# Attention with a mixer and an MLP on one core: which loads are issued in the opening, where the abs-max scans stand, and how the first normalized block is transposed

## The chip, the cores and the metric

The kernel runs on one core of a Trainium2 chip. The metric is the device time of one execution in microseconds. Five engines work beside each other: TensorE (PE, its weight loads PEld), VectorE (DVE), ScalarE (ACT), GpSimd (POOL) and SyncE (SP), whose sequencer here only issues DMAs. Each engine runs its instructions strictly in the order in which they stand in the program, and waits on semaphores where an operand comes from another engine or a DMA.

## The reference, cut to what matters

```python
xn = _layernorm(x)                       # x: 2048 tokens x 576
q = xn @ wq                              # 32 heads of 128
k, v = k_cache[:, :, -512:], v_cache[:, :, -512:]   # 16 key/value heads, two query heads each
p = softmax(q @ k.T * 128**-0.5)
s = concat_heads(p @ v) @ wo
h = gelu(_layernorm(xn) @ w1)            # four groups, shifted by 1, -1, 2, -2 tokens
x1 = xn + shifted(h) @ w2
g = silu(x1 + gelu(_layernorm(x1) @ w3) @ w4)
out = x + s * g
```

## The kernel before, in words

The program has two phases. The first (attention and mixer, lines 120 to 463) goes over four blocks of 512 tokens, and in each over 32 heads: 128 units u = 32·block + head. For every unit, `stage_q` projects the query (five matmuls of 128x512 into the tile `psq`, L242, copied to `qT` by ACT, L245), `stage_s` makes the scores of four key chunks (matmul `sc`, L254; exponential `pT` on ACT, L256; three PSUM buffers for `sc`), `stage_v` multiplies with the values (16 matmuls of 128x129 into `po`, two PSUM buffers, L269) and lets DVE divide by the sum (L272, L273) into `o`, which has three buffers, and `stage_t` transposes `o` by a DMA into `oT` (L280). In a step u the code calls `stage_q(u+1)`, `stage_s(u)`, `stage_v(u-1)`, `stage_t(u-2)`, and then what the table `fill` holds for that step: `at(u, fn)` puts it there. Through `fill` go the output projection of the block before (`wo_units`, 128 + 128 matmuls in the first steps of a block), the second layernorm (`ln2`), the mixer's first matmul and its gelu (`b1`: five times five matmuls `ph`, L334, with DVE and ACT work), its second (`b2`), the layernorm of the next block (`ln1`) and its DMA transposes (`tr1`), and loads.

The query weights pass through two buffers `wq_b`, each for four units: load j waits until the units that use the buffer's old slab have been projected. Keys (transposed by DMA, `kT`) and values (`v_sb`) are loaded once per key/value head, and stay. So do `wo_sb` (4.6 MB), `w1_sb` and `w2_sb`.

A guard runs beside this: the largest absolute value of every key head (`k_max`, L230, 16 reduces on DVE) and of each of the eight `wq` slabs (L438, 8 reduces of 128x2560) is combined by `finish_flag` into a flag, and a slow exact softmax follows if the bound is exceeded. It isn't with these inputs.

In the opening the code issues, on SP, four tiles of `x`, the first `wq` slab, keys and values of heads 0 and 1, the second slab, head 2; a GpSimd queue gets all of `wo` (L199) and then `w1` and `w2` (L204 to L213). `ln1(0)` and `tr1(0, .)` follow, then `stage_q(0)`.

The order within an engine is not the order of the code alone. A scheduler in the tile layer puts the instructions of each engine in order by its own estimate of when their operands are there; it may move a DVE reduce that the code has in step 20 ahead of the layernorm of the opening, if it reckons DVE idle there. What it made of the two programs is shown with the change.

The second phase (the MLP over four blocks, lines 466 on) loads its own weights and is not touched by the change.

Of the kernel before, what the change touches and what calls it, by code (L numbers as in the profile page):

```python
# [14 lines left out]
I32 = mybir.dt.int32  # L15

# [10 lines left out]
def kernel(  # L27
# [95 lines left out]
    with ExitStack() as actx:  # L123
# [16 lines left out]
        mx = res.tile([P, 8 + Hkv], FP32, name="mx")  # L140

# [40 lines left out]
        load_x(0, nc.sync)  # L182
        for w in wq_b:
            nc.gpsimd.memset(w[DR:, NF, :], 0.0)
        for w in xn_b + [xnn_b]:
            nc.gpsimd.memset(w[:, :, D:], 0.0)
        load_wq(0)
        load_kv(0)
        load_kv(1)
        nc.gpsimd.memset(v_sb[:, :, :, Dh:VW], 1.0)  # L190
        load_wq(1)
        load_kv(2)
# [4 lines left out]
        def load_wo():  # L197
            for h0 in range(0, Hq, 8):
                nc.gpsimd.dma_start(out=wo_sb[:, h0:h0 + 8, :],  # L199
                                    in_=A_wo[h0 * P:(h0 + 8) * P, :].rearrange("(h p) d -> p h d", p=P))  # L200

        def load_w12():
            for g in range(4):
# [7 lines left out]
                                    in_=B_w1[NF * P:D, g * c4 + P:(g + 1) * c4])  # L211
                nc.gpsimd.dma_start(out=w2_sb[:, g, :], in_=B_w2[g * c4:g * c4 + P, :])
# [23 lines left out]
        def stage_q(u):  # L236
            qb, h = divmod(u, Hq)
            w = wq_b[(u // 4) % NWQ]
            hh = h % 4
            psq = ps_pq.tile([P, QB], FP32, name="psq", tag="pq")  # L240
            for kc in range(NDC):
                nc.tensor.matmul(psq[:, :], lhsT=w[:, kc, hh * Dh:(hh + 1) * Dh], rhs=xnT_b[qb % 2][:, kc, :],  # L242
                                 start=(kc == 0), stop=(kc == NDC - 1))
            qT = qT_pool.tile([P, QB], BF16, name="qT")
            nc.scalar.activation(out=qT[:, :], in_=psq[:, :], func=ACT.Copy)  # L245
            qT_t[u] = qT
# [159 lines left out]
        for b in range(NB):  # L406
# [15 lines left out]
            if b + 1 < NB:  # L422
                at(base + 4, lambda b=b: load_x(b + 1, nc.gpsimd))
# [5 lines left out]
        at(2, load_wo)  # L429
        at(4, load_w12)  # L430
        for g in range(Hkv):
            if g + 3 < Hkv:
                at(2 * g, lambda g=g: load_kv(g + 3))
            at(2 * g + 2, lambda g=g: k_max(g))
        for j in range(2, NB * 8):
            at(4 * (j - 1), lambda j=j: load_wq(j))
        for j in range(8):
            at(4 * j + 1, lambda j=j: nc.vector.tensor_reduce(  # L438
                out=mx[:, j:j + 1], in_=wq_b[j % NWQ][:].rearrange("p a b -> p (a b)"), axis=AX.X, op=ALU.max,
                apply_absolute_value=True))  # L440
# [266 lines left out]
```

## Time and profile before

| | us |
|---|---|
| median of 3 runs | 969.01 (967.73 to 970.4) |
| the profiled execution: its own time | 967.13 |
| its span, from the first to the last instruction | 965.4 |
| TensorE busy | 866.0 (90%) |
| VectorE busy | 354.5 (37%) |
| ScalarE busy | 447.5 (46%) |
| first matmul | at 45.27 |

TensorE is the engine that is busy most, over all of the span but its opening. A busy share is read by stage: the windows view below gives it for each block of 32 units, and the waits view says what ended an engine's idle times.

### The profile page before, as it was taken

What the parts mean: (1) busy time and instruction counts of PE and PEld (TensorE: products, weight loads), DVE (VectorE), ACT (ScalarE), POOL (GpSimd) and SP (SyncE); (2) the same over time, 40 slices, a digit from 0 to 9 for tenths busy, and PEclk for the clock granted to TensorE, in tenths of its full rate; (3) what the DMA queues carried; (4) which work ended last, traced back from release to release, by engine and by line L of the source; (5) the groups of instructions that cost most, each with busy time, mean ns of one, the idle gap of its engine ahead of it and who ended that gap; (6) DMA issues with size and microseconds to landing.
All of it is one profiled execution on the core that took longest, in us unless ns stands there. A gap on an engine that the chain in (4) does not pass through costs nothing.

```text
span 965.4 us, 15852 instructions
## 1 busy us (share of the span) xinstructions
PE 866.0 (90%) x6356; PEld 468.6 (49%) x6356; DVE 354.5 (37%) x1145; ACT 447.5 (46%) x842; POOL 44.5 (5%) x84
## 2 busy tenths in 40 slices
PE   0168998999998999999999999957999999999996
PEld 0035554556555556556546555433444444444453
DVE  3567954212765212765203744300205104203012
ACT  0056686635767635768526767102223223224510
POOL 3510000000000000000000000010000000000000
PEclk9998999999999999999999999987999999999998
DMA  9985353303348303336403232439403103201001
GB/s 271 202 142 120 79 112 58 83 12 78 83 99 150 83 12 80 82 95 138 77 8 108 59 107 64 140 114 299 133 1 120 32 1 94 58 1 50 1 14 40
DMA packets 165648, 84.38 MB, mean 87 GB/s; under 512 B 122176, under 2 KB 163392, under 8 KB 165568
## 3 DMA queue, kind: packets, MB, share of 16 engines
q1 hardware_dynamic: 162160, 73.11, 32.9%
q0 software_dynamic: 3408, 10.19, 3.7%
q8 instruction: 52, 0.85, 0.4%
q14 instruction: 28, 0.23, 0.1%
HBM read 47.07 MB, written 9.44 MB: 59 GB/s over the span
## 4 chain that ended last, share of the span: by engine, by line
PE 71%; ACT 12%; SPq 5%; DMA 5%; issue 3%; DVE 3%; POOL 0%; DVEq 0%; ACTq 0%; POOLq 0%
PE ph L527 16%; PE pm L536 13%; PE psq L242 12%; PE pswo L296 12%; ACT qT L245 6%; PE po L269 6%; ACT pT L256 5%; PE sc L254 5%; DMA wq_b<-in_A_wq_dram 3%; SPq L178 2%; PE ph L334 2%; PE psx L370 2%; PE pr L537 2%; PE pswr L307 2%; DMA kT<-in_A_k_cache_dram 1%
## 5 line engine op out<-in xcount | busy, mean ns | idle before, releaser
L256 ACT ACTIVATE pT<-sc 128x512 bf16<-128x512 f32 x512 | 266.1, 609 | 5.7 <-PE sc L254 5.5
L242 PE MATMUL psq<-xnT_b,wq_b 128*128 128x512 bf16 x640 | 164.7, 386 | 45.8 <-DMA xnT_b<-xn_b 45.3
L527 PE MATMUL ph<-x1nT,w_s 128*128 128x512 bf16 x720 | 175.2, 384 | 15.0 <-DMA x1nT<-xm_b 15.0
L269 PEld LDWEIGHTS <-pT 128*128 128x128 bf16 x2048 | 140.9, 99 | 89.8 <-DVE o L273 25.6
L269 PE MATMUL po<-v_sb,pT 128*128 128x129 bf16 x2048 | 163.6, 222 | 20.2 <-DVE o L273 20.2
L254 PE MATMUL sc<-qT,kT 128*128 128x512 bf16 x512 | 155.3, 385 | 6.6
L530 ACT ACTIVATE h<-ph 128x512 bf16<-128x512 f32 x144 | 85.6, 596 | 156.1 <-PE ph L527 156.1
L536 PE MATMUL pm<-w_s,h 128*128 128x512 bf16 x576 | 155.0, 380 | 0.1
L245 ACT ACTIVATE qT<-psq 128x512 bf16<-128x512 f32 x128 | 76.4, 597 | 164.8 <-PE psq L242 164.7
L272 DVE RECIPROCAL ri<-po 128x2 f32<-128x2 f32 x256 | 42.9, 168 | 241.7 <-PE po L269 240.2
L296 PE MATMUL pswo<-wo_sb,oT 128*128 128x512 bf16 x512 | 113.2, 379 | 2.1 <-ACT s_out L299 2.1
L273 DVE TENSOR_TENSOR o<-po,ri 128x256 bf16<-128x256 f32 x256 | 107.7, 422 | 11.8 <-DMA oT<-o 5.4
L242 PEld LDWEIGHTS <-wq_b 128*128 128x128 bf16 x640 | 60.1, 99 | 105.2 <-issue 49.9
L527 PEld LDWEIGHTS <-w_s 128*128 128x128 bf16 x720 | 64.3, 99 | 90.8 <-DMA x1nT<-xm_b 15.1
L537 PE MATMUL pr<-w_s,h 128*128 128x64 bf16 x576 | 108.0, 193 | 0.0
L536 PEld LDWEIGHTS <-h 128*128 128x128 bf16 x576 | 56.2, 98 | 67.2
L545 DVE TENSOR_TENSOR bs<-pm,x 128x512 f32<-128x512 f32 x16 | 10.7, 686 | 205.3 <-PE pm L536 150.3
L296 PEld LDWEIGHTS <-oT 128*128 128x128 bf16 x512 | 49.4, 98 | 59.7 <-issue 2.9
L254 PEld LDWEIGHTS <-kT 128*128 128x128 bf16 x512 | 50.8, 99 | 47.5 <-issue 3.8
L537 PEld LDWEIGHTS <-h 128*128 128x128 bf16 x576 | 55.4, 98 | 12.7
L299 ACT ACTIVATE s_out<-pswo 128x512 bf16<-128x512 f32 x16 | 9.6, 597 | 105.4 <-PE pswo L296 105.4
L115 DVE BATCH_NORM_STATS2 ln_st<-x 128x6 f32<-128x288 bf16 x32 | 12.5, 431 | 72.7 <-DMA x<-x_dram 72.7
(77 smaller groups left out, 389.4 us busy)
## 6 DMA issues: line engine op xcount, KB each, us to landing
wq_b<-in_A_wq_dram SPq DMA_DIRECT2D x32, 512.0 KB, 3.9
w_s<-in_B_w_dram SPq DMA_DIRECT2D x9, 576.0 KB, 8.2
wo_sb<-in_A_wo_dram POOLq DMA_DIRECT2D x4, 1152.0 KB, 12.8
w_s<-in_B_w_dram SPq DMA_DIRECT2D x9, 512.0 KB, 7.9
s_dram<-s_out SPq DMA_DIRECT2D x4, 576.0 KB, 3.4
x_dram<-x1o SPq DMA_DIRECT2D x4, 576.0 KB, 3.5
s_b<-s_dram SPq DMA_DIRECT2D x4, 576.0 KB, 5.6
x_b<-in_A_x_dram SPq DMA_DIRECT2D x4, 576.0 KB, 6.3
```

Source lines behind the costliest of these rows:

```text
L242: nc.tensor.matmul(psq[:, :], lhsT=w[:, kc, hh * Dh:(hh + 1) * Dh], rhs=xnT_b[qb % 2][:, kc, :], start=(kc == 0), stop=(kc == NDC - 1))
L245: nc.scalar.activation(out=qT[:, :], in_=psq[:, :], func=ACT.Copy)
L254: nc.tensor.matmul(sc[:, :], lhsT=kT[:, g, kc * P:(kc + 1) * P], rhs=qT[:, :], start=True, stop=True)
L256: nc.scalar.activation(out=pT[:, :], in_=sc[:, :], func=ACT.Exp, scale=SCALE)
L269: nc.tensor.matmul(po[:, j, :], lhsT=pTs[kc][:, tt * P:(tt + 1) * P], rhs=v_sb[:, g, kc, 0:Dh + 1], start=(kc == 0), stop=(kc == KCH - 1))
L272: nc.vector.reciprocal(out=ri[:], in_=po[:, :, Dh])
L273: nc.vector.tensor_tensor(out=o[:, t0:t0 + 2, :], in0=po[:, :, 0:Dh], in1=ri[:].unsqueeze(2).to_broadcast([P, 2, Dh]), op=ALU.mult)
L296: nc.tensor.matmul(st["ps"][:, :], lhsT=oT_t[qb * Hq + h][:, tt, :], rhs=wo_sb[:, h, 0:M0], start=(h == 0), stop=(h == Hq - 1))
L527: nc.tensor.matmul(ph[:, :], lhsT=w3[:, kc, f0:f0 + P], rhs=x1nT[b % 2][:, kc, :], start=(kc == 0), stop=(kc == NDC - 1))
L530: nc.scalar.activation(out=h3[:, :], in_=ph[:, :], func=ACT.Gelu_apprx_tanh)
L536: nc.tensor.matmul(pm[tt][:, :], lhsT=lhsT, rhs=w4[:, fc % WS, 0:M0], start=(fc == 0), stop=(fc == FC - 1))
L537: nc.tensor.matmul(pr[:, tt, :], lhsT=lhsT, rhs=w4[:, fc % WS, M0:D], start=(fc == 0 and tt == 0), stop=(fc == FC - 1), skip_group_check=True)
```

## The change

The change orders the opening anew. (1) The `x` tiles of block 0 are issued half on SP and half on ACT. (2) The opening loads on SP are kept in the code's order (`manual_schedule`). (3) `wo` is cut into its four loads, issued at steps 5, 11, 17 and 23, `w1` at step 2, `w2` at step 20, the next block's `x` at step 17 in block 0. Each of these is gated by `late`: a copy of one element of that unit's `pT` on GpSimd, behind which the DMAs stand. (4) `k_max` and the `wq` scans are put into the steps of block 1, and `finish_flag` at step 68. (5) The transposes of block 0's normalized tokens are done by TensorE (`tr1_first`: 20 transposes of 128x128 in five PSUM tiles, copied out by DVE and ACT in turn). (6) In block 0 `qT` is copied out of PSUM by DVE instead of ACT.

```diff
+        def late(ap, fn):
+            g = nc.gpsimd.tensor_copy(out=gate[:, :], in_=ap)
+            with tc.issue_after(g.ins):
+                fn()
+
-        load_x(0, nc.sync)
+        x_t[0] = []
+        for tt in range(TB):
+            xt = xraw.tile([P, D], BF16, name="xt")
+            (nc.sync if tt < 2 else nc.scalar).dma_start(out=xt[:], in_=x2[tt * P:(tt + 1) * P, :])
+            x_t[0].append(xt)
...
-        load_wq(0)
-        load_kv(0)
-        load_kv(1)
-        load_wq(1)
-        load_kv(2)
+        with tc.manual_schedule(engines={SP}):
+            load_wq(0)
+            load_kv(0)
+            load_kv(1)
+            load_wq(1)
+            load_kv(2)
...
+        def tr1_first():
+            for kc, (cst, cw) in enumerate(DCH):
+                ps = ps_po.tile([P, QB], BF16, name="ps_x", tag="po")
+                for tt in range(TB):
+                    nc.tensor.transpose(out=ps[:, tt * P:(tt + 1) * P], in_=xn_t[0][:, tt, cst:cst + P],
+                                        identity=ident[:, :])
+                if kc % 2:
+                    nc.scalar.activation(out=xnT_b[0][:, kc, :], in_=ps[:, :], func=ACT.Copy)
+                else:
+                    nc.vector.tensor_copy(out=xnT_b[0][:, kc, :], in_=ps[:, :])
...
-            nc.scalar.activation(out=qT[:, :], in_=psq[:, :], func=ACT.Copy)
+            if qb == 0:
+                nc.vector.tensor_copy(out=qT[:, :], in_=psq[:, :])
+            else:
+                nc.scalar.activation(out=qT[:, :], in_=psq[:, :], func=ACT.Copy)
...
-                at(base + 4, lambda b=b: load_x(b + 1, nc.gpsimd))
+                at(base + (17 if b == 0 else 4), lambda b=b: late(pT_t[b * Hq + (17 if b == 0 else 4)][0][0:1, 0:1],
+                                                                 lambda: load_x(b + 1, nc.gpsimd)))
...
-        at(2, load_wo)
-        at(4, load_w12)
+        at(2, lambda: late(pT_t[2][0][0:1, 0:1], load_w1))
+        for i in range(4):
+            at(5 + 6 * i, lambda i=i: late(pT_t[5 + 6 * i][0][0:1, 0:1], lambda: load_wo(i)))
+        at(20, lambda: late(pT_t[20][0][0:1, 0:1], load_w2))
         for g in range(Hkv):
             if g + 3 < Hkv:
-                at(2 * g, lambda g=g: load_kv(g + 3))
-            at(2 * g + 2, lambda g=g: k_max(g))
+                at(2 * g + 1, lambda g=g: load_kv(g + 3))
+            at(Hq + 2 * g + 1, lambda g=g: k_max(g))
...
         for j in range(8):
-            at(4 * j + 1, lambda j=j: nc.vector.tensor_reduce(
+            at(Hq + 4 * j + 2, lambda j=j: nc.vector.tensor_reduce(
...
-        at(36, finish_flag)
+        at(2 * Hq + 4, finish_flag)
 
         ln1(0)
-        for tt in range(TB):
-            tr1(0, tt)
+        tr1_first()
```

What the scheduler made of it shows in three places. The first is the layernorm of block 0 on DVE, from its last statistics to the normalized tiles `xn`. Before (`L438` is a scan of a `wq` slab, `L230` one of a key head, `nr_` the steps of the inverse root):

```order
L96 TENSOR_SCALAR nr_y<-nr_v 128x4 [waits DVE_49]
L438 TENSOR_REDUCE mx<-wq_b_76 128x1 [waits DMAHW5_49,DMAHW4_49,Pool_49]
L100 TENSOR_TENSOR nr_t<-nr_y 128x4 [waits DVE_49]
L230 TENSOR_REDUCE mx<-kT 128x1 [waits DMAHW6_49]
L101 TENSOR_TENSOR nr_t<-nr_t,nr_v 128x4 [waits DVE_49]
L230 TENSOR_REDUCE mx<-kT 128x1 [waits DMAHW0_49]
L102 TENSOR_SCALAR nr_t<-nr_t 128x4 [waits DVE_49]
L104 TENSOR_TENSOR nr_y<-nr_y,nr_t 128x4 [waits DVE_49]
L100 TENSOR_TENSOR nr_t<-nr_y 128x4 [waits DVE_49]
L438 TENSOR_REDUCE mx<-wq_b_77 128x1 [waits DMAHW3_49,DMAHW2_49,Pool_49]
L101 TENSOR_TENSOR nr_t<-nr_t,nr_v 128x4 [waits DVE_49]
L230 TENSOR_REDUCE mx<-kT 128x1 [waits DMAHW4_49]
```

With the change:

```order
L116 BN_STATS ln_st<-xt 128x6
L256 TENSOR_REDUCE mx<-kT 128x1 [waits DMAHW6_49]
L117 BN_AGGR ln_mv<-ln_st 128x2 [waits DVE_49]
L95 TENSOR_SCALAR nr_v<-ln_mv 128x4 [waits DVE_49]
L97 TENSOR_SCALAR nr_y<-nr_v 128x4 [waits DVE_49]
L101 TENSOR_TENSOR nr_t<-nr_y 128x4 [waits DVE_49]
L256 TENSOR_REDUCE mx<-kT 128x1 [waits DMAHW0_49]
L102 TENSOR_TENSOR nr_t<-nr_t,nr_v 128x4 [waits DVE_49]
L103 TENSOR_SCALAR nr_t<-nr_t 128x4 [waits DVE_49]
L105 TENSOR_TENSOR nr_y<-nr_y,nr_t 128x4 [waits DVE_49]
```

The `wq` scans have left the layernorm (the eight now stand behind the quotients of units 25, 29, 33, 37, 41, 45, 49 and 54), and five of the seven key scans that stood within it; two are still there, and all sixteen key scans still stand in block 0, ahead of unit 6, although the code has them in block 1.

The second place is PE in a unit of block 0, from the last of the first three score matmuls on. Before (eight `po` matmuls stand between that `sc` and the fourth; the first five are shown):

```order
L254 LDWEIGHTS kT
L254 MATMUL sc<-qT,kT 128x512
L269 LDWEIGHTS pT
L269 MATMUL po<-v_sb,pT 128x129
L269 LDWEIGHTS pT
L269 MATMUL po<-v_sb,pT 128x129
L269 LDWEIGHTS pT
L269 MATMUL po<-v_sb,pT 128x129
L269 LDWEIGHTS pT
L269 MATMUL po<-v_sb,pT 128x129
L269 LDWEIGHTS pT
L269 MATMUL po<-v_sb,pT 128x129
```

With the change:

```order
L283 LDWEIGHTS kT
L283 MATMUL sc<-qT,kT 128x512
L298 LDWEIGHTS pT
L298 MATMUL po<-v_sb,pT 128x129
L298 LDWEIGHTS pT
L298 MATMUL po<-v_sb,pT 128x129
L298 LDWEIGHTS pT
L298 MATMUL po<-v_sb,pT 128x129
L298 LDWEIGHTS pT
L298 MATMUL po<-v_sb,pT 128x129
L283 LDWEIGHTS kT
L283 MATMUL sc<-qT,kT 128x512
```

The fourth score matmul stands behind four `po` matmuls now, and twelve follow it.

The third place is POOL's queue from the end of the opening's memsets. Before:

```order
L194 MEMSET w_sb 64x640 [waits Pool_49]
L199 DMA wo_sb<-in_A_wo_dram 128x8x576 x4
L167 DMA xt<-in_A_x_dram 128x576 [waits DMAHW0_49,DVE_49]
L167 DMA xt<-in_A_x_dram 128x576 [waits DMAHW1_49,DVE_49]
L167 DMA xt<-in_A_x_dram 128x576 [waits DMAHW2_49,DVE_49]
```

With the change, from the last of the 16 loads of `w1` on:

```order
L222 DMA w_sb<-in_B_w_dram 64x16 [waits DMASW7_49]
L185 COPY gate<-pT 1x1 [waits Activation_49,Pool_49]
L211 DMA wo_sb<-in_A_wo_dram 128x8x576 [waits DMASW0_49]
L185 COPY gate<-pT 1x1 [waits Activation_49,Pool_49]
L211 DMA wo_sb<-in_A_wo_dram 128x8x576 [waits DMASW1_49]
L185 COPY gate<-pT 1x1 [waits Activation_49,Pool_49]
L169 DMA xt<-in_A_x_dram 128x576 [waits DMAHW0_49,DMASW2_49,DVE_49]
```

The four `wo` loads stood at once behind the memsets; each now stands behind a copy that waits for ACT.

## Rows read from the trace of the kernel before

**Rows 1.** The page: TensorE's busy tenths in 40 slices of the span

```profile
PE   0168998999998999999999999957999999999996
```

**Rows 2.** Who waited for whom, whole run: us in total, times, longest

```profile
PE psq L242 <- DMA xnT_b<-xn_b: 45.3, 1, 45.3
...
PE po L269 <- DVE o L273: 20.2, 8, 5.3
```

**Rows 3.** Timeline of the opening: start, us, engine, line, op; idle before and releaser

```profile
5.25 3.71 POOL L199 DMA_DIRECT2D wo_sb<-in_A_wo_dram  x4
5.65 1.18 SPq L178 DMA_TRANSPOSE kT<-in_A_k_cache_dram  x1
18.53 0.69 DVE L230 TENSOR_REDUCE mx<-kT 128x1 f32<-128x512 bf16 x1 [6.49 <-DMA kT<-in_A_k_cache_dram]
19.33 0.16 DVE L104 TENSOR_TENSOR nr_y<-nr_y,nr_t 128x4 f32<-128x4 f32 x1
19.53 0.16 DVE L100 TENSOR_TENSOR nr_t<-nr_y 128x4 f32<-128x4 f32 x1
26.95 2.82 DVE L438 TENSOR_REDUCE mx<-wq_b 128x1 f32<-128x2560 bf16 x1 [7.27 <-DMA wq_b<-in_A_wq_dram]
33.76 1.45 DVE L119 TENSOR_SCALAR xn_b<-xt,ln_mv,nr_y 128x576 bf16<-128x576 bf16 x4
45.27 4.43 PE L242 MATMUL psq<-xnT_b,wq_b 128*128 128x512 bf16 x10 [45.27 <-DMA xnT_b<-xn_b]
```

**Rows 4.** Key loads: landing times of the first two, and of one issued at 27.97

```profile
DMA to landing us min/median/max: 5.0/8.9/12.9
...
DMA to landing us min/median/max: 2.7/2.7/2.7
```

**Rows 5.** Windows of blocks 0 and 1, line L242 alone: length, PE busy, PEld, PEclk, DMA, GB/s

```profile
45.26:172.54 127.28, 44.11 (x160) 15.45 (x161) 0.95 0.55 104
172.54:317.07 144.53, 40.86 (x160) 14.93 (x161) 0.99 0.39 84
```

**Rows 6.** Timeline of one plain unit in block 2, PE and ACT

```profile
382.49 1.24 PE L242 MATMUL psq<-xnT_b,wq_b 128*128 128x512 bf16 x5
383.57 0.81 PE L254 MATMUL sc<-qT,kT 128*128 128x512 bf16 x3
...
384.91 0.38 PE L254 MATMUL sc<-qT,kT 128*128 128x512 bf16 x1
...
385.59 0.38 PE L242 MATMUL psq<-xnT_b,wq_b 128*128 128x512 bf16 x1
...
383.77 0.60 ACT L245 ACTIVATE qT<-psq 128x512 bf16<-128x512 f32 x1 [0.54 <-PE psq L242]
384.26 2.06 ACT L256 ACTIVATE pT<-sc 128x512 bf16<-128x512 f32 x4
```

**Rows 7.** Timeline of block 0: two `wq` scans, and the `po` matmuls behind them

```profile
67.21 2.82 DVE L438 TENSOR_REDUCE mx<-wq_b 128x1 f32<-128x2560 bf16 x1 [4.65 <-DMA wq_b<-in_A_wq_dram]
70.62 1.92 PE L269 MATMUL po<-v_sb,pT 128*128 128x129 bf16 x16 [5.34 <-DVE o L273]
99.75 2.82 DVE L438 TENSOR_REDUCE mx<-wq_b 128x1 f32<-128x2560 bf16 x1 [0.65 <-DMA wq_b<-in_A_wq_dram]
102.96 0.64 PE L269 MATMUL po<-v_sb,pT 128*128 128x129 bf16 x8 [0.61 <-DVE o L273]
```

**Rows 8.** Windows: around the first of these waits (PE, PEld, DVE, ACT, POOL; PEclk, DMA, GB/s)

```profile
68.10:74.90 6.80, 4.28 (x26) 2.90 (x26) 5.37 (x21) 1.47 (x4) 0.00 (x0) 0.50 0.17 34
```

**Rows 9.** Windows: block 0, all engines

```profile
45.26:172.54 127.28, 107.66 (x789) 62.30 (x790) 82.91 (x272) 82.47 (x160) 10.28 (x17) 0.95 0.55 104
```

**Rows 10.** Groups by line in block 0: busy us, mean ns

```profile
L230 DVE TENSOR_REDUCE mx<-kT 128x1 f32<-128x512 bf16 x7 | 4.7, 677 | 10.0 <-DMA kT<-in_A_k_cache_dram 10.0
L337 DVE CAST g_x<-ph 128x512 bf16<-128x512 f32 x5 | 3.4, 682 | 0.0
...
L115 DVE BATCH_NORM_STATS2 ln_st<-xn_b 128x6 f32<-128x288 bf16 x8 | 3.2, 429 | 0.0
```

More of the change, by code (lines that the diff above doesn't have):

```diff
@@ L15 @@
 I32 = mybir.dt.int32
+SP = mybir.EngineType.SP
 LN_EPS = 1e-5
@@ L140 @@
         mx = res.tile([P, 8 + Hkv], FP32, name="mx")
+        gate = res.tile([1, 1], BF16, name="gate")
         oT_pool = pool("oT_pool", 36)
@@ L180, in load_kv @@
                               in_=A_v_cache[0, g, K0:, :].rearrange("(kc p) d -> p kc d", p=P))
-        load_x(0, nc.sync)
+        def late(ap, fn):
[7 more added lines that the diff above has]
+            x_t[0].append(xt)
+        for w in xn_b + [xnn_b]:
+            nc.gpsimd.memset(w[:, :, D:], 0.0)
         for w in wq_b:
             nc.gpsimd.memset(w[DR:, NF, :], 0.0)
-        for w in xn_b + [xnn_b]:
-            nc.gpsimd.memset(w[:, :, D:], 0.0)
-        load_wq(0)
-        load_kv(0)
-        load_kv(1)
+        with tc.manual_schedule(engines={SP}):
[4 more added lines that the diff above has]
+            load_kv(2)
         nc.gpsimd.memset(v_sb[:, :, :, Dh:VW], 1.0)
-        load_wq(1)
-        load_kv(2)
         nc.gpsimd.memset(w1_sb[:, :, 4 * P:], 0.0)
@@ L195, with load_wo, load_w1 @@
         nc.gpsimd.memset(w2_sb[:, 4, :], 0.0)
[L197 to L202, printed above, removed]
+        def load_wo(i):
+            h0 = i * 8
+            nc.gpsimd.dma_start(out=wo_sb[:, h0:h0 + 8, :],
+                                in_=A_wo[h0 * P:(h0 + 8) * P, :].rearrange("(h p) d -> p h d", p=P))
+        def load_w1():
             for g in range(4):
@@ L211, in load_w12, with load_w2 @@
                                     in_=B_w1[NF * P:D, g * c4 + P:(g + 1) * c4])
+        def load_w2():
+            for g in range(4):
                 nc.gpsimd.dma_start(out=w2_sb[:, g, :], in_=B_w2[g * c4:g * c4 + P, :])
```

## The prediction

> **What bounds the kernel now.** I read the page's slices first: TensorE is busy in nine tenths or more of nearly every slice, except at the start, in a few slices of block 0, and at the seam of the two phases [rows 1]. The change touches the start, block 0 and block 1. Next, the view of who waited for whom: TensorE's one great wait is 45.3 us for the DMA transposes of the first normalized block, and after it 20.2 us, in eight waits, for DVE's quotient `o`, which frees `po`'s buffers [rows 2]. The timeline of the opening tells why the first wait is so long. DVE has the layernorm's statistics early, but the scheduler put scans between its small steps: one of a key head idles DVE 6.49 us for its load, one of the second `wq` slab another 7.27 us, and `xn` is written only at 33.76 [rows 3]. The loads are late because 4.6 MB of `wo` were issued at 5.25, beside them: the key load at 5.65 took 12.9 us to land, the one before it 5.0, and one at 27.97, with `wo` done, 2.7 [rows 3, 4]. From `xn` to the first matmul another 10 us pass in DMA transposes [rows 3].
>
> Then block 0. A plain unit takes 385.59 - 382.49 = 3.10 us [rows 6]; five `b1` groups add five matmuls of 0.216 each, 5.4 in all. So 32 units would take 104.6, but the window has 127.28 [rows 5]: **22.7 us are lost inside block 0**. Some 18 of it are waits for `o` behind `wq` scans, whose slab had not landed [rows 2, 7]; the rest is the slow clock. The first ten matmuls stand 443 ns apart, the pitch of 1.2 GHz [rows 3], and after a wait of 5.34 us the granted clock was 0.50, again 1.2 GHz, for 6.8 us [rows 7, 8].
>
> **The opening, step by step.** Two of the four `x` issues leave SP, so the key loads are issued 0.9 earlier, the second at 4.7. Two key scans are left in the layernorm. The first key load, with no `wo` beside it, lands within 5.0 [rows 4], by 7.8; its scan (0.68 [rows 10]) and four small steps bring DVE to 9.3. The second scan waits for the load of 4.7. The trace of before has no such load without `wo` beside it and with 1.2 MB of `x` and `wq` ahead: its bounds are 2.7 and 12.9 [rows 4]. I take 5.0, that of its neighbour, since `wo` is gone: 9.7, and 10.4 after the scan. Eleven small steps at 0.2 (19.33 to 19.53 [rows 3]) end at 12.6, `xn` (1.45 [rows 3]) at 14.05.
>
> From there TensorE makes 20 transposes. The nearest row has 16 matmuls of 129 columns in 1.92 [rows 7], 0.12 each, so 2.4 us; they go beside DVE, whose queue holds, up to the last of its three copies, six statistics of 0.43 [rows 10], two aggregates of some 0.2, and the copies, for which I take the cast of 0.68 [rows 10]: 2.6 + 0.4 + 2.0 = 5.0. The last chunk is there at 19.1. The last matmul of unit 0 and five of unit 1 follow at 0.443, so the projection of the two units ends at 21.8; before, at 45.27 + 4.43 = 49.7 [rows 3]. **The opening gives 27.9.** With the second key load at its bounds it gives 30.2 or 20.0. The Trainium skill, "VectorE: DVE Perf Modes", section "The three transpose paths", has 390 ns for a 128x128 transpose on TensorE; one after another that would be 7.8 us, 2.8 more than DVE's 5.0, and by it the time would be that much longer. No run here shows such a transpose yet.
>
> **Block 0 and block 1 together** took 127.28 + 144.53 = 271.8 [rows 5]. Of the terms, in order:
>
> *The qT copy on DVE.* Now ACT's copy starts at 383.77 and holds the first exponential back to 384.26; 0.65 later the fourth score matmul gets its buffer, at 384.91, where TensorE, by 383.57 + 3·0.216 + 8·0.058, could have gone at 384.69 [rows 6]. Without the copy the exponential would start at 383.99 and the matmul would not wait: 0.22 a unit. But the changed order puts that matmul behind four `po` instead of eight. TensorE is there at 384.45 and waits to 383.99 + 0.65 = 384.64; then twelve `po` follow. The unit ends 0.216 + 12·0.058 later, at 385.55: 3.05 for 3.10. **Over 32 units 1.4 us**, not 7.
>
> *The loss inside block 0* of 22.7 goes, and is replaced by these. The slow start stays: ten matmuls at 443 for 216 ns, 2.3. The `wq` scans move, and each still stands close behind the issue of its slab, which waits until unit 4k+3, the last on its buffer, has been projected; the scan stands ahead of the quotient of unit 4k+2, which TensorE makes possible one unit, 3 us, later. Two of the eight (after units 33 and 37) have the output projection beside them and cost nothing; two stand beside `b1` or `b2` work, like the one at 99.75 that cost 0.61 [rows 7]; four stand in plain units, at a price between 0.61 and 5.34 [rows 7], for which I take the mean of the eight waits, 20.2/8 = 2.5 [rows 2]. That makes 11.2, with bounds of 3.7 and 22.6. `finish_flag`, whose round trip through DRAM cost one more such wait, moves from block 0 to block 1 and costs 2.5 again.
>
> *New waits in block 0.* DVE, busy 82.91 there [rows 9], loses 6·2.82 of scans, and gets 32 casts of 0.68, seven key scans of 0.68 and two `wq` scans: 98 us in some 115. It keeps up on the average, not always: in units 0 to 5 it has 14 key scans and the second layernorm beside the quotients (I charge 1 us), in `b1`'s five units 3.9 of DVE work to 4.1 of TensorE's (2 us). The gated `x` loads of block 1 are issued in unit 17 and wanted by DVE in that unit (1 us). The `wo` loads now pass beside the `oT` transposes, which free `o` (2 us). In all 6, between 0 and the 18 that the old scans cost.
>
> So the two blocks take 271.8 - 22.7 - 1.4 + 2.3 + 11.2 + 2.5 + 6 = 269.7, a gain of 2.1. What the change saves there by the casts and by moving the scans is nearly given back. Blocks 2, 3 and the second phase stay: their loads and order are the same. The gates on POOL cost nothing where their units leave slack: `w1` is issued in unit 2 and wanted in unit 11, the last `wo` in unit 23 and wanted in unit 34; if a gate slipped ten units, the first `wo` matmuls would wait.
>
> **Sum:** 27.9 + 2.1 = 30.0. Against the profiled execution's 967.1 that is 937.1. It took 1.9 less than the median; from the median of 969.0 it is 939.0. I forecast 938, between the two.
>
> **Rivals.** (a) *The layernorm still waits for its second key load as now*, 12.9 us after its issue, and the scans cost their upper bound: + 7.9 + 11.4, 957. For it: 1.2 MB stand before that load in the same queue. Against: the load before it, behind nearly the same bytes, took 5.0. (b) *DMA is calm once `wo` is spread*, slabs land before their scans and nothing new waits: - 7.5 - 6, 925. For it: a key load took 2.7 in calm; against: the scan stands where the slab can hardly be there. (c) **Slower:** *DVE, full in block 0, stalls TensorE so long that the clock falls.* A wait like that of rows 7 costs 5.34 and half of the 6.8 at 0.50 [rows 8], 8.7 us. Four more of them than I charge bring back 35 and the kernel is at 973; from there on the change loses. For it: 98 of 115 us, and casts that wait for a projection with quotients queued behind. Against: every cast stands in TensorE's own order, a unit before its scores. (d) *The change doesn't do what it says*: in part that is so, since the key scans stay in block 0; it is in the sum. If the first transposes waited as the DMA's did, the opening would end 5 us later: 943.
>
> **Chances.** The forecast with its bounds 0.74, (a) 0.12, (b) 0.09, (c) 0.04; 0.01 for gains and losses that cancel. No change within 0.3% (2.9 us, about what a measurement of this kernel can tell) lies between (a) and (c). Faster 0.94, the same 0.02, slower 0.04. The range reaches down to a little below (b), and up to (a): 921 to 957.
>
> **What would show it.** In the new profile the first projection matmul at 16 to 20 us and none of TensorE's waits over 7 us after it; DVE's scan of the second key head at about 9.7; plain units of block 0 at 3.05; `qT` on DVE near 0.68; PE's waits for `o` of some 15 to 20 us in all, now after units 25, 29, 41 and 54. Wrong it would be if TensorE's first matmul came after 25, if plain units of block 0 took more than 3.3, or if blocks 2 and 3 changed by more than 2 us.

## The result, and the profile after

The changed kernel takes **936.26 us** (median of four, 935.56 to 937.65); beside it the kernel before took 968.42 (four, 967.73 to 970.4). The ratio is 0.9667, with a 95% interval of 0.9647 to 0.9686. The forecast was 938 in 921 to 957. The profiled execution has a span of 933.7, 31.7 less than before.

The page of the changed kernel, its first line and TensorE's busy tenths:

```profile
span 933.7 us, 15814 instructions
...
PE   4799889999969999999999999939999999999996
```

Against [rows 1] the empty start is shorter by more than a slice (a slice is some 23 us), and there are still dips in the first half.

To see where the time went I cut both spans at the first exponential of units 0, 32 and 64, and at that of the last unit, 127: what lies ahead is the opening, then come block 0, block 1, blocks 2 and 3 together, and the second phase. First the windows of the kernel before (line L256 alone: start and end, length, ACT's busy time and count, granted clock, DMA share, GB/s), then those of the kernel after (its line L285):

```profile
50.22:177.41 127.19, 66.67 (x128) 0.95 0.52 101
177.41:321.95 144.54, 66.64 (x129) 0.99 0.39 84
321.95:604.11 282.16, 130.71 (x252) 1.00 0.32 75
604.11:965.40 361.29, 2.11 (x5) 0.97 0.26 73
```

```profile
19.77:137.99 118.22, 66.87 (x128) 0.96 0.82 166
137.99:291.62 153.63, 66.44 (x129) 0.99 0.37 79
291.62:573.78 282.16, 130.72 (x253) 1.00 0.33 77
573.78:933.70 359.92, 2.11 (x5) 0.97 0.25 73
```

So the opening gave 50.22 - 19.77 = 30.5 us, block 0 gave 9.0, **block 1 took 9.1 back**, blocks 2 and 3 did not move, and the second phase gave 1.4; 31.7 in all, by unrounded times. This cut is the measure in every experiment below, and "behind unit u" means between the first exponentials of units u and u + 1.

The opening, from the timeline of the kernel after (start, us, engine, line, operation; idle before it and what ended that):

```profile
4.74 1.17 SPq L180 DMA_TRANSPOSE kT<-in_A_k_cache_dram  x1
...
7.75 0.69 DVE L256 TENSOR_REDUCE mx<-kT 128x1 f32<-128x512 bf16 x1 [0.72 <-DMA kT<-in_A_k_cache_dram]
...
9.07 0.68 DVE L256 TENSOR_REDUCE mx<-kT 128x1 f32<-128x512 bf16 x1
...
11.84 1.45 DVE L120 TENSOR_SCALAR xn_b<-xt,ln_mv,nr_y 128x576 bf16<-128x576 bf16 x4
...
12.33 1.41 PE L245 MATMUL ps_x<-ident,xn_b 128*128 128x128 bf16 x8 [12.33 <-DVE xn_b L120]
...
13.67 0.42 DVE L250 COPY xnT_b<-ps_x 128x512 bf16<-128x512 bf16 x1
...
14.15 0.58 PE L245 MATMUL ps_x<-ident,xn_b 128*128 128x128 bf16 x4 [0.41 <-DVE xnT_b L250]
...
14.53 1.06 PE L268 MATMUL psq<-xnT_b,wq_b 128*128 128x512 bf16 x2
...
16.24 3.24 PE L268 MATMUL psq<-xnT_b,wq_b 128*128 128x512 bf16 x8
...
16.48 0.42 DVE L250 COPY xnT_b<-ps_x 128x512 bf16<-128x512 bf16 x1
```

Two key scans are still in the layernorm. The first waits 0.72 us for its load; the second, at 9.07, has no wait in front of it, where the second of before idled DVE for 6.49 [rows 3]. The `wq` scan that idled it for 7.27 is gone from there, and `xn` is written from 11.84 instead of 33.76. TensorE's projections begin at 14.53, among its own transposes, and end at 16.24 + 3.24 = 19.5.

Two units of block 0 after its `b1` groups, from the same timeline, lie 85.75 - 82.70 = 3.05 apart, against 3.10 in [rows 6]; DVE's copy of `qT` takes 0.69:

```profile
82.70 0.81 PE L283 MATMUL sc<-qT,kT 128*128 128x512 bf16 x3
...
85.75 0.81 PE L283 MATMUL sc<-qT,kT 128*128 128x512 bf16 x3
...
85.95 0.69 DVE L272 CAST qT<-psq 128x512 bf16<-128x512 f32 x1 [0.32 <-PE psq L268]
```

Who waited for whom, in the kernel after (us in total, times, longest), the rows that answer to [rows 2] and those on DVE behind them:

```profile
PE po L298 <- DVE o L302: 21.3, 12, 4.1
...
DVE mx L470 <- DMA wq_b<-in_A_wq_dram: 18.2, 8, 4.6
...
PE ph L558 <- DMA x1nT<-xm_b: 14.0, 1, 14.0
...
DVE o L302 <- DMA oT<-o: 11.2, 6, 4.5
...
DVE mx L256 <- DMA kT<-in_A_k_cache_dram: 2.0, 2, 1.3
```

TensorE still waits as long for `o` as before (21.3 for 20.2). Behind that stand two causes on DVE: scans that wait for a slab, and quotients that wait for the `oT` transpose which frees `o`'s buffer.

### The profile page after: what moved, and what is told of

It is laid out like the page before. It is cut to its first block, busy times and chain, and to the rows that moved or that the text cites. A ratio compares the mean times of both kernels' runs of the same rounds, so it can differ in the third digit from the quotient of the medians.

```text
span 933.7 us, 15814 instructions
## 1 busy us (share of the span) xinstructions
PE 860.9 (92%) x6266; PEld 469.7 (50%) x6376; DVE 376.5 (40%) x1180; ACT 433.4 (46%) x812; POOL 46.0 (5%) x93
## 4 chain that ended last, share of the span: by engine, by line
PE 69%; issue 13%; ACT 9%; DMA 5%; DVE 3%; SPq 1%; POOL 0%; DVEq 0%; ACTq 0%; POOLq 0%
PE ph L558 16%; PE pm L567 13%; PE psq L268 11%; PE pswo L325 10%; PE po L298 7%; PE sc L283 6%; ACT qT L274 4%; ACT pT L285 4%; PE pr L568 2%; PE ph L363 2%; DMA oT<-o 2%; PE psx L399 1%; DMA kT<-in_A_k_cache_dram 1%; PE pswr L336 1%; DMA wq_b<-in_A_wq_dram 1%
## 5 line engine op out<-in xcount | busy, mean ns | idle before, releaser
L285 ACT ACTIVATE pT<-sc 128x512 bf16<-128x512 f32 x512 | 266.1, 607 | 58.1 <-PE sc L283 58.0
L558 PE MATMUL ph<-x1nT,w_s 128*128 128x512 bf16 x701 | 173.5, 383 | 15.1 <-DMA x1nT<-xm_b 14.0
L298 PEld LDWEIGHTS <-pT 128*128 128x128 bf16 x2048 | 140.9, 99 | 91.3 <-DVE o L302 27.1
L298 PE MATMUL po<-v_sb,pT 128*128 128x129 bf16 x2048 | 164.4, 222 | 21.3 <-DVE o L302 21.3
L283 PE MATMUL sc<-qT,kT 128*128 128x512 bf16 x512 | 153.4, 381 | 6.6 <-ACT pT L285 0.9
L268 PE MATMUL psq<-xnT_b,wq_b 128*128 128x512 bf16 x600 | 156.3, 386 | 2.3 <-issue 0.2
L567 PE MATMUL pm<-w_s,h 128*128 128x512 bf16 x557 | 152.2, 380 | 0.2
L301 DVE RECIPROCAL ri<-po 128x2 f32<-128x2 f32 x256 | 42.4, 167 | 194.5 <-PE po L298 193.3
L302 DVE TENSOR_TENSOR o<-po,ri 128x256 bf16<-128x256 f32 x256 | 107.5, 422 | 17.4 <-DMA oT<-o 11.2
L274 ACT ACTIVATE qT<-psq 128x512 bf16<-128x512 f32 x96 | 57.3, 597 | 78.3 <-PE psq L268 78.1
```

The source lines that it names most:

```text
L283: nc.tensor.matmul(sc[:, :], lhsT=kT[:, g, kc * P:(kc + 1) * P], rhs=qT[:, :], start=True, stop=True)
L285: nc.scalar.activation(out=pT[:, :], in_=sc[:, :], func=ACT.Exp, scale=SCALE)
L298: nc.tensor.matmul(po[:, j, :], lhsT=pTs[kc][:, tt * P:(tt + 1) * P], rhs=v_sb[:, g, kc, 0:Dh + 1], start=(kc == 0), stop=(kc == KCH - 1))
L301: nc.vector.reciprocal(out=ri[:], in_=po[:, :, Dh])
L302: nc.vector.tensor_tensor(out=o[:, t0:t0 + 2, :], in0=po[:, :, 0:Dh], in1=ri[:].unsqueeze(2).to_broadcast([P, 2, Dh]), op=ALU.mult)
L558: nc.tensor.matmul(ph[:, :], lhsT=w3[:, kc, f0:f0 + P], rhs=x1nT[b % 2][:, kc, :], start=(kc == 0), stop=(kc == NDC - 1))
```

## The experiments

Each kernel is the changed one with the edit shown. Medians are of four executions; the ratio is to the kernel before on the same chip, whose median lay between 965.33 and 968.42, so a difference of two medians from different chips is good to some 3 us. "Block 0" and "block 1" are the stretches between first exponentials. Parts (1) and (2) of the change, the `x` tiles on two queues and the fixed order on SP, were not undone by themselves.

| kernel | us | ratio (95%) | first exponential | block 0 | block 1 |
|---|---|---|---|---|---|
| changed | 936.26 | 0.9667 (0.9647 to 0.9686) | 19.77 | 118.22 | 153.63 |
| first_by_dma | 950.95 | 0.9815 (0.9773 to 0.9857) | 24.46 | 125.54 | 156.38 |
| loads_ungated | 949.11 | 0.9811 (0.9777 to 0.9844) | 20.96 | 129.38 | 154.02 |
| wo_at_once | 942.87 | 0.9763 (0.9714 to 0.9812) | 34.89 | 108.82 | 155.32 |
| no_scans | 919.59 | 0.9510 (0.9479 to 0.9541) | 17.88 | 116.37 | 140.78 |
| scans_pinned | 919.78 | 0.9522 (0.9475 to 0.9569) | 18.31 | 117.59 | 140.93 |
| scans_as_before | 933.45 | 0.9640 (0.9599 to 0.9680) | 25.54 | 126.81 | 137.96 |
| qT_on_act | 948.26 | 0.9816 (0.9764 to 0.9868) | 18.43 | 132.43 | 154.32 |
| o_six | 934.03 | 0.9659 (0.9628 to 0.9690) | 19.97 | 117.13 | 152.26 |
| pinned_o6 | 915.68 | 0.9484 (0.9436 to 0.9533) | 17.58 | 112.87 | 140.92 |
| v_on_act | 911.35 | 0.9419 (0.9382 to 0.9457) | 22.66 | 103.39 | 140.91 |
| v_on_act_qT_act | 916.92 | 0.9490 (0.9441 to 0.9538) | 23.68 | 106.73 | 140.94 |
| v_paced | 911.20 | 0.9432 (0.9389 to 0.9475) | 18.08 | 110.40 | 140.92 |

### What made the opening short

**wo_at_once**: the four `wo` loads back at the start, everything else as changed.

```diff
+        g0 = nc.gpsimd.memset(v_sb[:, :, :, Dh:VW], 1.0)
+        with tc.issue_after(g0.ins):
+            for i in range(4):
+                load_wo(i)
...
-        for i in range(4):
-            at(5 + 6 * i, lambda i=i: late(pT_t[5 + 6 * i][0][0:1, 0:1], lambda: load_wo(i)))
```

> The changed kernel with the four wo loads issued at once on POOL, at some 4 us, ahead of w1; w1, w2 and x stay gated, and SP's order, transposes and scans are as changed. Theory A (wo beside the key loads set the opening before the change): the second key load lands about 12.9 us after its issue, xn starts at some 19 to 20 instead of 11.8; 8 us are lost in the opening, some 4 come back where wo would have been late: 938 to 946. Theory B (SP's order put the first two key loads ahead of wo's traffic, and wo hits a later load instead, as in the run without gates): xn starts at 12 to 14, but a key load of units 0 to 4 takes over 8 us to land and block 0 loses it: 940 to 950.

DVE's second key scan and two issues in SP's queue, from the timeline of this kernel:

```profile
8.41 5.29 SPq L175 DMA_DIRECT2D wq_b<-in_A_wq_dram  x1
13.74 6.09 SPq L177 DMA_DIRECT2D wq_b<-in_A_wq_dram  x1
```

```profile
24.80 0.69 DVE L260 TENSOR_REDUCE mx<-kT 128x1 f32<-128x512 bf16 x1 [15.23 <-DMA kT<-in_A_k_cache_dram]
```

Theory A holds, and is too small: the scan waits 15.23 us, and the opening loses 15.1. So `wo` beside the key loads delays the layernorm by that much. But block 0 is 9.4 us shorter than in the changed kernel: the spread `wo` loads cost block 0 about that much. (About, because the longer opening also lets SP issue more key and value loads ahead of block 0.) The net worth of moving `wo` is 942.87 - 936.26 = 6.6 by the medians, not the whole opening.

**loads_ungated**: every gate taken away.

```diff
         def late(ap, fn):
-            g = nc.gpsimd.tensor_copy(out=gate[:, :], in_=ap)
-            with tc.issue_after(g.ins):
-                fn()
+            fn()
```

> The changed kernel without the gates: wo, w1, w2 and the x of block 1 are issued as soon as POOL is free; order of SP, transposes and scans as changed. Theory A (the gates set the opening): the second key load lands some 12.9 us after its issue, as before the change, so xn starts at 20 or later instead of 11.8 and the opening loses 8 to 9 us; the wait of 4.7 us behind unit 26, beside late weights, goes; in all 936.3 + 4, 940 (938 to 946). Theory B (the order of SP's queue sets the opening and the gates do nothing): xn starts at 12 to 13, the wait behind unit 26 goes, the time is 931 to 935.

Neither fits whole. POOL's order put `w1` first here, so `wo` was issued from 16.87 on, and the opening lost only 1.2. It then hit a key load in SP's queue, whose issue alone took 11.42 us, and DVE's scan of a key head waited 10.64:

```profile
20.43 11.42 SPq L180 DMA_TRANSPOSE kT<-in_A_k_cache_dram  x1
...
37.49 0.69 DVE L254 TENSOR_REDUCE mx<-kT 128x1 f32<-128x512 bf16 x1 [10.64 <-DMA kT<-in_A_k_cache_dram]
```

Block 0 lost 11.2, though the wait behind unit 26 went, as theory B had it. With the run before it, this says that `wo`'s 4.6 MB hurt whatever DVE or TensorE wants next from SP's queue, in the opening or behind it.

**first_by_dma**: the first block transposed by DMA again.

```diff
-        tr1_first()
+        for tt in range(TB):
+            tr1(0, tt)
```

> The changed kernel with the first block transposed by four DMA transposes, as before the change; all else as changed. Theory A (TensorE's transposes are a term of their own in the opening): the four DMA transposes stand in SP's queue beside the key loads; the first projection matmul comes at 20 to 22 us instead of 14.5, and the time is 5 to 8 us over the changed kernel's 936.3. Theory B (the 10 us from xn to the first matmul before the change were wo's contention alone): with wo gated the transposes land within some 4 us of xn, the first projection matmul comes at about 17 and the time is 2 to 3 us over.

```profile
11.65 1.45 DVE L120 TENSOR_SCALAR xn_b<-xt,ln_mv,nr_y 128x576 bf16<-128x576 bf16 x4
12.16 5.20 SPq L239 DMA_TRANSPOSE xnT_b<-xn_b  x4
...
19.03 4.43 PE L268 MATMUL psq<-xnT_b,wq_b 128*128 128x512 bf16 x10 [19.03 <-DMA xnT_b<-xn_b]
```

The opening is 4.7 longer, near theory A's 5, with the first projection at 19.0. The rest of the 14.7 was foreseen by neither. The four transposes hold SP's queue for 5.2 us, so the key loads come later; and the scheduler now has ten key scans ahead of DVE's first quotient, where the changed kernel has seven. DVE's key scans wait, by this row of the waits, in nine places instead of two, and how much of that either cause makes is not shown:

```profile
DVE mx L256 <- DMA kT<-in_A_k_cache_dram: 20.7, 9, 5.4
```

### What the scans cost

**no_scans**: without the scans and the flag (set to zero).

```diff
-            at(Hq + 2 * g + 1, lambda g=g: k_max(g))
...
-            at(Hq + 4 * j + 2, lambda j=j: nc.vector.tensor_reduce(
...
-        at(2 * Hq + 4, finish_flag)
+        nc.vector.memset(flag_i[:], 0)
```

> The changed kernel without the abs-max scans of keys and wq and without the flag worked out from them (it is set to zero): this run leaves that part out. Theory A (the scans, waiting on DVE for slabs in front of quotients, are the waits that the changed kernel shows behind units 28, 44, 47 to 49, 56, 57 and 59, 17.4 us beyond the plain periods): these go, and the opening gains the two key scans and the wait for a key, 2.1: 916 to 918. Theory B (the slabs are late whoever waits for them, because SP's queue is held up by transposes, and TensorE would wait for the slab or the oT transposes instead): 926 to 932.

The windows of blocks 0 and 1 (columns as above):

```profile
17.88:134.25 116.37, 66.77 (x129) 0.96 0.83 171
134.25:275.03 140.78, 66.47 (x129) 1.00 0.40 86
```

16.7 us by the medians, short of theory A by some 2: the opening gives 1.9 and block 1 12.9, but block 0 only 1.9. Of its waits the one behind unit 28 is gone; those of units 5 to 8 and 26 are still there, and now `o`'s wait for its transposes is 26.7 us in all.

**scans_pinned**: all scans kept, but each queued behind a quotient that comes after its data (`o_i[u]` is the last quotient of unit `u`).

```diff
+        def behind(v, fn):
+            with tc.issue_after(o_i[v]):
+                fn()
...
-            at(Hq + 2 * g + 1, lambda g=g: k_max(g))
+            at(Hq + 2 * g + 1, lambda g=g: behind(Hq + 2 * g, lambda: k_max(g)))
...
-            at(Hq + 4 * j + 2, lambda j=j: nc.vector.tensor_reduce(
+            at(Hq + 4 * j + 2, lambda j=j: behind(Hq + 4 * j + 1, lambda: nc.vector.tensor_reduce(
```

> The changed kernel with each scan queued on DVE behind a quotient that comes after its data: key head g behind the quotient of unit 32+2g, wq slab j behind that of unit 33+4j. Nothing is left out. Theory A (a scan costs by the load that it waits for in front of quotients, and next to nothing by its own 2.82 or 0.68 us): block 1 falls from 153.6 to 142 to 144, the wait behind unit 28 goes, the opening gains 1.9 as in the run without scans: 920 to 923. Theory B (DVE's own time is the price, 22.6 us of wq scans and 10.8 of key scans in a block whose quotients TensorE waits for): block 1 stays at 150 or more: 928 to 934.

```profile
18.31:135.90 117.59, 66.77 (x129) 0.96 0.85 168
135.90:276.83 140.93, 66.33 (x129) 1.00 0.38 83
```

Theory A: with the same 24 scans in block 1 it takes 140.93, against 140.78 without any. **In block 1 the scans cost by what they wait for in front of quotients, and nothing that shows by their own time**, on a DVE that is busy for 94.5 of those 140.9 us. The changed kernel's text puts them in block 1, but without an edge that holds them there its order had the key scans in block 0, two of them in the layernorm, and each `wq` scan ahead of its slab.

**scans_as_before**: the scans written at their old units.

```diff
-            at(Hq + 2 * g + 1, lambda g=g: k_max(g))
+            at(2 * g + 2, lambda g=g: k_max(g))
...
-            at(Hq + 4 * j + 2, lambda j=j: nc.vector.tensor_reduce(
+            at(4 * j + 1, lambda j=j: nc.vector.tensor_reduce(
...
-        at(2 * Hq + 4, finish_flag)
+        at(36, finish_flag)
```

> The changed kernel with the scans written at the units where they stood before the change (wq slab j at unit 4j+1, key head g at 2g+2, the flag at unit 36); loads, gates, transposes and casts as changed. Theory A (what the scans cost depends on the load that each waits for and what stands behind it, and the change moved only the wq scans): two wq scans of 2.82 and the second slab's landing stand ahead of xn again, so the opening loses 5 to 8; block 0 pays for six wq scans, 10 to 18; block 1 falls from 153.6 to some 144: 942 to 952. Theory B (the scans' waits are the same sum wherever they stand): block 0 gains what block 1 loses, 934 to 939.

```profile
25.54:152.35 126.81, 66.38 (x128) 0.93 0.72 145
152.35:290.31 137.96, 66.47 (x128) 1.00 0.41 91
```

Each stretch moved the way that theory A said (opening + 5.8, block 0 + 8.6, block 1 - 15.7), block 0 by less than its 10 to 18 and block 1 by more than its 9.6, and the sum is theory B's: 933.45, an interval that overlaps the changed kernel's. I had not counted that block 1, rid of the scans, falls below the 144.5 of before. Part of that is work that only moved: 13 of the 128 output projection matmuls of 0.216, 2.8 us, stand in block 0 here, where the changed kernel has none. The opening shows what a scan costs where DVE itself is waited for: two `wq` scans of 2.82 and two more key scans of 0.68 stand ahead of `xn`, none of these four waits for its load, and `xn` starts at 17.96 instead of 11.84. **As it was made, the move of the scans gained nothing that these runs can tell.**

### The cast of qT

**qT_on_act**: ACT copies `qT` in block 0 too.

```diff
-            if qb == 0:
-                nc.vector.tensor_copy(out=qT[:, :], in_=psq[:, :])
-            else:
-                nc.scalar.activation(out=qT[:, :], in_=psq[:, :], func=ACT.Copy)
+            nc.scalar.activation(out=qT[:, :], in_=psq[:, :], func=ACT.Copy)
```

> The changed kernel with ACT copying qT in block 0 too, as in the other blocks. Theory A (the copy on DVE buys the 0.04 us a unit that the prediction worked out, and no more): plain units of block 0 at 3.10 instead of 3.06, b1 units at 4.17 instead of 4.14, time 936.3 + 1.2, 937 to 938. Theory B (DVE is crowded in units 2 to 8 by the casts, so the waits there come partly from them): plain units at 3.10, but the waits of 7.0 us behind units 5 to 8 shrink by half: 933 to 935.

Both theories miss: 12 us slower, and block 0 alone is 14.2 longer. The row of the waits that changed most says where:

```profile
DVE mx L256 <- DMA kT<-in_A_k_cache_dram: 19.9, 9, 9.4
```

Plain units are at 3.09 to 3.10, as worked out. But with the casts gone from DVE the key scans stand earlier among its instructions, ahead of loads that had not landed. The edit's own price can't be read from this run; it was tried again on a kernel without such waits (below).

### The wait that is left: SP's queue

**o_six**: six buffers for `o`.

```diff
-        o_pool = pool("o_pool", 3)
+        o_pool = pool("o_pool", 6)
```

> The changed kernel with six buffers for the quotient o instead of three. Theory A (o's buffers are held by oT transposes that wait in SP's queue behind key loads and block transposes, and nothing else is late there): the waits behind units 5 to 8 (7.0 us beyond the plain period) and 26 (4.7) go: 924 to 926. Theory B (SP's queue itself is full there, and the wait only moves, to the block transposes for b1, to a slab or to a key load): 932 to 936.

Theory B: 934.03, not told apart from the changed kernel. The wait went from `o`'s buffers to the next scan of a key whose load stood in the same queue:

```profile
45.92 0.69 DVE L256 TENSOR_REDUCE mx<-kT 128x1 f32<-128x512 bf16 x1 [3.72 <-DMA kT<-in_A_k_cache_dram]
```

**pinned_o6**: scans_pinned, and with it

```diff
-        o_pool = pool("o_pool", 3)
+        o_pool = pool("o_pool", 6)
```

> The last kernel with six buffers for o as well. Theory A (six buffers gained only 2 us because key scans in front of quotients took over the wait at unit 7; with these gone SP's queue has slack on the average and the buffers ride over it): the waits behind units 5 to 8 and 26 shrink to some 3 us in all: 910 to 914. Theory B (SP's queue is full through units 4 to 9, and a slab or key load is what comes late): within 3 us of the last kernel.

Between the two: 4.1 us less than scans_pinned. The waits of units 5 to 8 are gone, that of unit 26 is 1.4 instead of 4.5, but a new one has come, for a slab whose load SP issued only at 51.46, behind key and value loads and `oT` transposes. From the first exponential to 60 us, 42.4 us, SP's issues take 39.4 (in the changed kernel 36.7 of 40.2):

```profile
51.46 0.53 SPq L175 DMA_DIRECT2D wq_b<-in_A_wq_dram  x1
```

```profile
55.66 2.32 PE L273 MATMUL psq<-xnT_b,wq_b 128*128 128x512 bf16 x5 [6.89 <-DMA wq_b<-in_A_wq_dram]
```

**v_on_act**: pinned_o6, and ACT issues the values from head 3 on.

```diff
-            nc.sync.dma_start(out=v_sb[:, g, :, 0:Dh],
+            (nc.sync if g < 3 else nc.scalar).dma_start(out=v_sb[:, g, :, 0:Dh],
```

> The kernel with pinned scans and six o buffers, with the value loads from head 3 on issued by ACT instead of SP. Theory A (SP's queue holds the load of the fourth wq slab back behind key and value loads, so TensorE waits 6.9 us for it, and with the value loads gone, some 8 us of issue, the slab is issued in time): the long period at unit 10 goes, block 0 takes 103 to 106 instead of 112.9, time 905 to 909. Theory B (the DMA engines are what is full there, and the slab lands as late): 913 to 917.

The windows of block 0 in pinned_o6 and here:

```profile
17.58:130.45 112.87, 66.55 (x128) 0.97 0.94 174
```

```profile
22.66:126.05 103.39, 66.44 (x129) 1.00 0.89 179
```

ACT's issues of values over the run (count; ns: shortest, median, longest), and the start of its queue:

```profile
L181 ACTq DMA_DIRECT2D v_sb<-in_A_v_cache_dram x13: 374/394/520, 0.8 to 22.2; - x13
```

```profile
2.28 13.34 ACTq L181 DMA_DIRECT2D v_sb<-in_A_v_cache_dram  x10
15.65 1.28 ACT L248 ACT_TABLE_LOAD   x1 [15.65 <-DMA v_sb<-in_A_v_cache_dram]
```

Theory A for block 0: it is free of waits but for some 1 us at unit 26. That alone does not say whether the queue or the DMA engines were full, since part of the traffic left block 0: by length times rate it moved 18.5 MB, against 19.6 in pinned_o6, and the opening 4.8 (212 GB/s) against 3.5 (198 GB/s). The next run tells the two apart.

The opening lost 5.1. ACT got to its first copy of a transposed block only behind 15.65, and it was not its issues that took so long: each took 0.37 to 0.52 us. Between them ACT waited for landings. In this program the loads of SP and ACT together signal their landing on eight semaphores, and an issue waits until the earlier load on its semaphore has landed: the last of the ten issues begins at 15.24, and the value load before it on that semaphore, issued at 9.94, landed at 15.22.

The Trainium skill, "DMA: Bandwidth & Descriptors", section "Issuing engines are not separate DMA queues", says that starting DMAs from several engines saves only the time to initiate them, "which is usually small relative to the DMA itself". The trace agrees for one load: the issue of a value load takes 0.58 us in pinned_o6, and it lands 3.2 us behind its issue, by the medians. But SP's issues stand one behind another, and there the sum of them is nearly all of the time.

**v_paced**: the same loads, each behind the last exponential of an odd unit (`p_i[u]`).

```diff
+            if g < 3:
+                load_v(g, nc.sync)
+            else:
+                with tc.issue_after(p_i[2 * g - 5]):
+                    load_v(g, nc.scalar)
```

> The kernel with the value loads on ACT, each now queued behind the last exponential of an odd unit instead of all at the start (value head g behind unit 2g-5). Theory A (with all eleven issued at once, ACT was held in its own queue until 15.6 us, so its copies of the first transposed block came late, and the opening lost 5 us; SP's relief of 9.5 us in block 0 stays): first exponential at 17.5 to 18.5 us instead of 22.7, block 0 at 103 to 104: 905 to 908. Theory B (the key transposes, thirteen in a row on SP, take the DMA engines in the opening, whoever issues the values): first exponential at 21 or later: 910 to 912.

(ACT got thirteen value loads, not eleven.) The opening is as theory A had it, 18.08, but the time is 911.20, as of v_on_act: block 0 took 110.40. The exponentials are late by 3.73 in the row below and by 4.38 at another place, and TensorE waits 2.77 and 3.41 for them:

```profile
37.61 0.41 ACTq L180 DMA_DIRECT2D v_sb<-in_A_v_cache_dram  x1
38.07 2.06 ACT L297 ACTIVATE pT<-sc 128x512 bf16<-128x512 f32 x4 [3.73 <-DMA wq_b<-in_A_wq_dram]
```

The scores were there, and the issue itself took 0.41. ACT stood in front of it until the slab load before it on the same semaphore had landed, at 30.59 + 7.0 = 37.59:

```profile
30.59 1.07 SPq L177 DMA_DIRECT2D wq_b<-in_A_wq_dram  x1
```

```profile
DMA to landing us min/median/max: 7.0/7.0/7.0
```

So the value load, and with it the exponentials, waited for a slab that neither of them reads. At the other place it was the landing of a block transpose, at 107.80, with the issue at 107.82.

Block 0 also tells the queue from the engines:

```profile
18.08:128.48 110.40, 66.45 (x129) 0.98 0.93 182
```

```profile
41.38 0.58 SPq L175 DMA_DIRECT2D wq_b<-in_A_wq_dram  x1
```

It moved 20.1 MB, more than pinned_o6 did, at about the same DMA share, and TensorE still waits at most 0.2 us for a slab. The slab that came late there is issued 41.38 - 18.08 = 23.3 us behind the first exponential here, against 51.46 - 17.58 = 33.9. So it was SP's queue, and not the DMA engines, that was full.

**v_on_act_qT_act**: v_on_act, and with it

```diff
-            if qb == 0:
-                nc.vector.tensor_copy(out=qT[:, :], in_=psq[:, :])
-            else:
-                nc.scalar.activation(out=qT[:, :], in_=psq[:, :], func=ACT.Copy)
+            nc.scalar.activation(out=qT[:, :], in_=psq[:, :], func=ACT.Copy)
```

> The last kernel with ACT copying qT in block 0 as in the other blocks, with scans pinned and no queue in the way. Theory A (the cast's worth is the 0.04 us a unit of the prediction; the 12 us that its undoing cost the changed kernel came from the key scans that the scheduler then put ahead of the first quotients): plain units 3.10 instead of 3.06, b1 units 4.17 instead of 4.14, 1.0 to 1.5 us slower than the last kernel. Theory B (the cast on DVE is worth more, since ACT, with qT, is late for exponentials in block 0): 4 us or more slower.

```profile
23.68:130.41 106.73, 66.53 (x129) 1.00 0.86 172
```

Block 0 is 3.3 longer. Plain units are at 3.09 to 3.10 for 3.06, and 32 units at 0.03 to 0.04 make 1.1, as theory A says; two single waits, behind units 6 and 19, make most of the rest. In the medians it is 5.6, with intervals that overlap. So the cast is worth about 1 us by itself; what else came with it was more than that in this execution, and why it came is not shown.

v_on_act and v_paced are the fastest kernels here, each some 25 us under the changed one by their medians, 2.6% and 2.4% by their ratios.

## Why the prediction was right

**The opening**: 27.9 forecast. To the end of the first two projections, which is what the forecast counted, it gave 49.7 - 19.5 = 30.2 (30.5 to the first exponential). That this is the forecast's upper bound is luck. The bound was summed wrongly: with the second key load in 2.7 us DVE would still reach that scan only at 9.3, 0.4 earlier and not 2.3, so the bound should have been 28.3, and the measured value lies above it. The mechanism held: second key scan at 9.07 (forecast 9.7), `xn` from 11.84 (12.6), first projection at 14.53 (16 to 20), last chunk at 16.48 + 0.42 = 16.9 (19.1), projections done at 19.5 (21.8). Two terms were too dear: the second key load landed 4.0 us after its issue, not 5.0, and a copy of `ps_x` took DVE 0.42, not the 0.68 of the cast, so DVE's way from the end of `xn` to the last chunk was 16.9 - 13.3 = 3.6, not 5.0. The copy reads bf16 where the cast reads f32. That agrees with the Trainium skill, "VectorE: DVE Perf Modes", section "Why PSUM operands drop a tier", by which an f32 operand in PSUM runs at a lower rate than other PSUM operands. The 390 ns that the Trainium skill has for a transpose on TensorE (same page, section "The three transpose paths") did not show as a pitch: a transpose takes 0.31 us by itself, but the next one starts some 0.11 behind it. Undone one at a time, the place of `wo`, the transposes and the place of the scans give back 15.1, 4.7 and 5.8 of the 30.5; what makes the rest was not tried.

**The plain unit** of block 0: 3.05 forecast, 3.05 to 3.06 measured. The cause holds too: with ACT copying `qT` again it is 3.09 to 3.10 (v_on_act_qT_act).

**The scans**: 11.2 for the scans and 2.5 for the flag were charged; blocks 0 and 1 together lose 14.7 without them (271.85 against 257.15). They fell where the forecast had them: the scans behind the quotients of units 25, 41, 45 and 54 show as waits behind units 28, 44, 47 and 56 (the one of unit 29 cost 0.6). They were dearer in plain units (4.0 behind unit 28, 4.6 behind 56), and 1.4 and 2.3 beside `b1` instead of 0.61, with nothing beside the output projection; the flag cost 2.8, behind unit 59. Of TensorE's waits for `o`, 21.3 us in all for the 15 to 20 forecast, 11.9 lie behind scans and flag and 8.6 in units 5 to 8 and 26.

**New waits in block 0**: 6 forecast. This is the term that was mis-sized. Without scans the two blocks still take 257.15, and 244.30 in v_on_act, where SP's queue is relieved and `o` has six buffers, so 12.9 lay there (in that kernel the scans are there, held where they cost nothing; its opening is 4.8 longer than without scans). The step that failed is "The `wo` loads now pass beside the `oT` transposes, which free `o` (2 us)": the edit that made the opening short put all of `wo` into block 0, at 9.4 us by the run with `wo` at once, and in SP's queue key loads, value loads, block transposes, slabs and `oT` transposes stand in one row, which I had priced nowhere.

**Blocks 0 and 1** together were to gain 2.1 and lost 0.1: the waits were 7.9 dearer than charged (14.7 + 12.9 for 13.7 + 6), but block 1 of before had 3.8 of its own (144.54 against 140.78, a quotient that waited 3.96 for an `oT` transpose) that I had left in the sum and that went, and the slow start, 2.3, lies ahead of the first exponential, in the opening; **blocks 2 and 3** are the same to 0.01 us, as forecast. **The second phase** gained 1.4 that I had not counted; its wait for `x1nT` went from 15.0 to 14.0. In the twelve kernels of the experiments, whose second phase is the same code, it takes 359.3 to 360.6, so part of the 1.4 is such scatter; why the rest went is open. So the error of 1.7 in the sum of 30.0 is made of 2.6 too little in the opening, 2.2 too much in the blocks and 1.4 missed, up to rounding: the sum is better than its terms.

**The rivals**: (a) and (b) didn't come. (c)'s wait behind the scans is real, but the longest wait for `o` was 4.1 us, not 5.34, and block 0's granted clock stayed at 0.96. (d)'s price for the first transposes, 5 us, was 4.7 in the opening.

## What to carry to other kernels

A large early load costs whatever is wanted next from the same DMA engines, so spread it; but then count, queue by queue, what it passes beside: here 9.4 of 15.1 us came back as waits. Before loads are moved to a second engine, look which semaphores they share with those of the first: here exponentials waited for the landing of loads that they do not use. An operation written late in the program is not late on its engine unless an edge holds it there: 24 scans cost 16 us in one order and nothing that these runs can tell in another. When a part of a change is undone to price it, read first whether the rest of the order stayed; here undoing a cast worth 1 us cost 12.

## What the runs showed of the hardware

- A DMA issue can hold the engine that makes it. A key load's issue on SP took 1.17 us in the changed kernel's opening and 11.42 with `wo` under way. (ACT's 13.34 us for ten value loads were waits for landings between issues of 0.37 to 0.52 us.)
- Transposes of 128x128 bf16 on TensorE took 0.31 us each and stood some 0.11 us apart (eight in 1.06), before the clock had risen.
- A copy of 512 columns out of PSUM on DVE took 0.42 from bf16 and 0.69 from f32; on ACT 0.60 from either.
- The eight projections behind the transposes took 3.24 us and stood 0.427 us apart up to 18.80, where those from 20.00 on stand 0.216 apart: the pitches of the levels of 1.2 and 2.4 GHz, as the ten in [rows 3], 0.427 apart by their starts, and the later ones of that kernel. The trace has its first record of the granted clock at 18.97, with 1.00. A windows row shows 1.00 for time without a record too, so there the pitch tells the level, and not the row.
